# Transposes on TensorE whole or as pairs of 64-row blocks, and a new order of the operations

## The chip, the cores and the metric

The kernel runs on one core of one Trainium2 chip. The metric is the device time of one execution in microseconds; lower is better. The times of the kernel before are 197.99, 198.35 and 198.89 us, with a median of 198.35.

## The reference

Two stages follow each other. The first is a linear attention with a state of 40 x 40 for each of 4 batches and 8 heads over 768 steps; the second mixes tokens and channels of its output.

```python
for t in range(S):                                  # (B, H, S, D) = (4, 8, 768, 40)
    y[:, :, t] = np.einsum('bhd,bhde->bhe', rt, state)
    Sa = np.einsum('bhde,bhe->bhd', state, at)
    state_decay = state * wt[:, :, None, :] - np.einsum('bhd,bhe->bhde', Sa, bt)
    state = state_decay + np.einsum('bhd,bhe->bhde', vt, kt)
x = y.transpose(0, 2, 1, 3).reshape(B, S, H * D)    # (4, 768, 320)
theta = x @ w_theta
zr, zi = x * np.cos(theta), x * np.sin(theta)
u = x + np.einsum('ts,bsd->btd', w_tok_r, zr) + np.einsum('ts,bsd->btd', w_tok_i, zi)
out = u + np.maximum(u @ w_ch, 0.0)
```

## The kernel before

The 768 steps of a batch are cut into 6 chunks of 128 tokens, 24 chunks in all, numbered through the batches. For each chunk the kernel loads w, k, b, a, v and r (160 KB each), takes the logarithm of w on ACT (`lw`, L445), sums it over the chunk with a triangular matmul, and scales k, b and a with the exponentials (`kb` and `ah`, mostly on POOL). The scaled tiles are transposed on PE against an identity (`tkb`, `ta`, `tv`, `tr`, `to`, `tb`, and later `nut`, `xt`, `ut`, `wt`): a transpose is a matmul whose output lies in PSUM, and ACT or DVE copies it out (`ekb`, `ea`, `ev` and so on).

From the transposed tiles PE makes four score tiles for each chunk (`spsi`, `sphi`, `slv`, `slu`, L569). A score matmul contracts over 64 rows only, so two heads stand side by side in the upper and lower 64 rows of PE's array, each with a PSUM bank of its own. DVE multiplies a score tile with a mask (L578), or ACT copies it and POOL masks it. The recurrence of a chunk is then two steps, x0 (L616) and nu (L629), with a copy `nx` between them, a new state `gt` (L652), its transpose `gd` and the chunk's output y (L800, L802). The second stage adds theta, its sine and cosine (on ACT), the products z, the token mixing (`row`, L881, six steps of two 320-column matmuls a chunk) and the channel mixing (L763, L773). The token weights come as 12 tiles `wrow` of 128 x 768, loaded by DMAs that POOL issues (L960).

Nothing in this order comes from the loops. Each operation is recorded by `plan.add` with its number, what it reads and writes, and, where another engine could do it, an alternative (`alts`). Three tables decide: `ORDER` is the order in which all 1602 operations are issued, and since each engine works through its own instructions in order, it is the order on each engine and on SP's queue of loads and stores; `PICK` lists the operations that take their alternative; `HOMES` gives each PSUM tile its bank. PSUM has 8 banks. Banks 0 to 3 form two doubles (`ps_d`) for score tiles, and banks 4 to 7 are singles (`ps_s`) for all else:

```python
doubles = [psum.tile([128, 2, 512], FP32, name=f"ps_d{i}") for i in range(DOUBLE // 2)]
singles = [psum.tile([128, 512], FP32, name=f"ps_s{i}") for i in range(BANKS - DOUBLE)]
```

A fourth table, `WARM`, puts matmuls on a constant tile (`busy`, L1019) ahead of a few early operations. All but 11 of the 134 recorded transposes go through PE; the 11 of `CROSSBAR` are done by DMA.

Of the kernel before, what the change touches and what calls it, by code (L numbers as in the profile page):

```python
# [26 lines left out]
    0, 7, 3, 6, 1, 2, 20, 8, 21, 23, 24, 4, 27, 9, 32, 30, 5, 22, 31, 33, 12, 25, 26, 34, 11,  # L27
    28, 10, 69, 35, 36, 29, 70, 37, 18, 47, 44, 40, 19, 48, 72, 45, 38, 41, 71, 49, 73, 39, 46,
    98, 119, 76, 99, 58, 14, 42, 100, 74, 57, 15, 13, 120, 122, 101, 50, 121, 79, 75, 51, 123,
    53, 106, 102, 107, 131, 108, 80, 52, 16, 77, 109, 132, 125, 78, 43, 103, 81, 17, 110, 134,  # L30
    126, 111, 133, 82, 56, 84, 137, 54, 104, 124, 138, 112, 129, 83, 85, 87, 130, 88, 127, 55,
    156, 86, 128, 59, 157, 89, 146, 184, 143, 90, 147, 105, 158, 61, 97, 60, 139, 187, 159,
    135, 62, 144, 148, 164, 96, 188, 160, 165, 191, 140, 93, 136, 145, 161, 166, 141, 91, 185,
    167, 213, 186, 92, 194, 214, 149, 189, 142, 162, 168, 150, 215, 163, 169, 190, 216, 195,
    152, 221, 170, 234, 151, 246, 192, 222, 235, 193, 237, 217, 95, 236, 202, 238, 218, 94,
    196, 203, 197, 63, 241, 155, 247, 171, 267, 248, 219, 239, 199, 198, 172, 220, 223, 205,
    249, 200, 240, 271, 64, 244, 272, 242, 299, 245, 201, 154, 273, 224, 243, 300, 173, 301,
    261, 206, 254, 274, 302, 225, 174, 262, 303, 279, 153, 175, 258, 306, 176, 255, 212, 259,
    263, 280, 250, 177, 204, 281, 256, 211, 275, 496, 282, 260, 320, 226, 251, 305, 257, 208,
    252, 276, 264, 283, 253, 317, 207, 227, 349, 327, 265, 277, 497, 328, 304, 309, 278, 329,  # L40
    498, 284, 266, 310, 270, 499, 330, 350, 285, 307, 351, 268, 318, 286, 354, 308, 269, 331,
    352, 500, 311, 361, 332, 319, 287, 314, 353, 312, 209, 336, 333, 539, 362, 210, 337, 289,
    356, 288, 315, 363, 313, 322, 290, 364, 338, 355, 291, 387, 325, 292, 339, 316, 365, 540,
    388, 359, 366, 389, 541, 357, 360, 340, 390, 341, 382, 358, 391, 321, 116, 503, 113, 501,
    542, 412, 373, 181, 342, 334, 376, 374, 502, 392, 367, 411, 326, 504, 377, 375, 506, 335,
    393, 368, 505, 323, 178, 369, 545, 524, 394, 378, 370, 507, 517, 525, 413, 508, 372, 526,
    384, 371, 509, 395, 416, 396, 527, 532, 417, 528, 397, 510, 511, 514, 529, 544, 117, 595,
    512, 572, 533, 415, 383, 530, 118, 398, 573, 515, 596, 513, 554, 385, 399, 534, 531, 574,
    418, 597, 401, 535, 400, 516, 575, 414, 402, 543, 379, 324, 404, 114, 567, 598, 536, 403,
    546, 548, 115, 380, 581, 642, 576, 582, 555, 601, 549, 577, 381, 583, 599, 66, 386, 550,  # L50
    584, 537, 557, 568, 600, 551, 182, 522, 558, 602, 183, 585, 586, 538, 619, 578, 561, 587,
    419, 179, 518, 559, 547, 604, 519, 556, 427, 180, 428, 421, 429, 605, 560, 420, 606, 520,
    423, 552, 607, 626, 553, 562, 434, 422, 627, 564, 435, 425, 436, 565, 563, 643, 628, 424,
    437, 644, 610, 566, 629, 426, 613, 645, 603, 588, 611, 630, 231, 523, 571, 521, 589, 438,
    430, 570, 698, 635, 631, 646, 612, 439, 431, 636, 632, 440, 608, 745, 432, 614, 699, 647,
    609, 746, 700, 675, 648, 747, 637, 433, 615, 676, 616, 701, 293, 569, 633, 677, 748, 634,
    651, 649, 638, 678, 590, 652, 684, 296, 579, 685, 679, 617, 639, 228, 620, 621, 580, 653,
    706, 657, 591, 654, 680, 592, 618, 686, 650, 593, 661, 703, 687, 594, 441, 622, 711, 702,
    640, 442, 681, 712, 662, 688, 655, 658, 705, 656, 689, 659, 641, 663, 660, 682, 704, 664,
    690, 749, 667, 683, 665, 691, 68, 709, 692, 707, 67, 710, 729, 668, 65, 670, 672, 666, 708,  # L60
    694, 693, 750, 624, 695, 730, 719, 713, 697, 751, 720, 731, 696, 232, 732, 294, 233, 297,
    714, 721, 295, 733, 738, 298, 229, 734, 739, 715, 716, 230, 740, 735, 717, 754, 450, 752,
    451, 778, 755, 718, 346, 625, 452, 779, 453, 741, 343, 623, 756, 881, 780, 454, 757, 408,
    882, 781, 742, 405, 673, 671, 764, 883, 767, 765, 669, 782, 884, 444, 722, 455, 783, 443,
    768, 456, 766, 445, 784, 446, 736, 457, 885, 785, 458, 760, 737, 743, 447, 459, 753, 448,
    786, 787, 887, 744, 761, 796, 788, 769, 758, 460, 759, 789, 763, 461, 888, 762, 790, 462,
    797, 912, 463, 792, 791, 913, 793, 723, 770, 795, 892, 771, 914, 794, 674, 893, 915, 886,
    772, 802, 890, 464, 891, 803, 773, 347, 465, 916, 348, 344, 799, 917, 905, 805, 409, 345,
# [133 lines left out]
def mm(n):  # L202
    return max(n / 2.4 + 2.5, 25.0)
# [853 lines left out]
```

## Time and profile before

| | |
|---|---|
| median of the runs | 198.35 us |
| profiled execution, first to last instruction | 197.8 us |
| PE busy | 187.6 us (95%), 3288 matmuls |
| DVE busy | 164.3 us (83%) |
| ACT busy | 151.7 us (77%) |
| POOL busy | 145.1 us (73%) |
| HBM read and written | 29.54 MB and 3.93 MB |

Busy times of PE count a matmul from its start to its modelled end, so matmuls overlap. In a row of the chain of waits stand the start, the length and what took the time; the chain runs back from the last instruction to what released each one. A row of groups gives the count, the busy time, the mean of one in ns, and the idle time before it with what ended it.

### The profile page before, as it was taken

What the parts mean: (1) busy time and instruction counts of PE and PEld (TensorE: products, weight loads), DVE (VectorE), ACT (ScalarE), POOL (GpSimd) and SP (SyncE); (2) the same over time, 40 slices, a digit from 0 to 9 for tenths busy, and PEclk for the clock granted to TensorE, in tenths of its full rate; (3) what the DMA queues carried; (4) which work ended last, traced back from release to release, by engine and by line L of the source; (5) the groups of instructions that cost most, each with busy time, mean ns of one, the idle gap of its engine ahead of it and who ended that gap; (6) DMA issues with size and microseconds to landing.
All of it is one profiled execution on the core that took longest, in us unless ns stands there. A gap on an engine that the chain in (4) does not pass through costs nothing.

```text
span 197.8 us, 8019 instructions
## 1 busy us (share of the span) xinstructions
PE 187.6 (95%) x3288; PEld 150.3 (76%) x3288; DVE 164.3 (83%) x261; ACT 151.7 (77%) x337; POOL 145.1 (73%) x210
## 2 busy tenths in 40 slices
PE   7888999999989999999999999999999999999992
PEld 6776787777768788878878888888887878767661
DVE  5269899999989999888887988999999988675453
ACT  3584979799889988979988598888998986575111
POOL 8267544679879999699799939769699697558100
PEclk9999999999999999999999999999999999999999
DMA  6999879989999999999998899988998274863055
GB/s 119 210 212 163 154 161 196 182 166 197 233 174 173 207 171 185 190 185 223 153 210 168 153 187 170 188 148 169 182 155 163 43 177 102 87 194 104 0 191 174
DMA packets 134644, 32.75 MB, mean 166 GB/s; under 512 B 124816, under 2 KB 134608, under 8 KB 134608
## 3 DMA queue, kind: packets, MB, share of 16 engines
q1 hardware_dynamic: 131680, 29.19, 75.1%
q0 software_dynamic: 2784, 2.97, 9.6%
q8 instruction: 25, 0.41, 0.9%
q10 hardware_dynamic: 144, 0.08, 0.1%
q14 instruction: 11, 0.09, 0.1%
HBM read 29.54 MB, written 3.93 MB: 169 GB/s over the span
## 4 chain that ended last, share of the span: by engine, by line
PE 68%; DMA 9%; ACT 8%; SPq 6%; DVE 3%; issue 3%; POOL 1%; ACTq 0%; DVEq 0%; POOLq 0%
PE ps_s L881 17%; PE ps_s L391 10%; PE ps_d L569 9%; PE ps_s L763 5%; SPq L409 4%; DMA raw_w<-in_w_dram 3%; DMA raw_kb<-in_k_dram 3%; PE ps_s L711 3%; PE ps_s L652 2%; PE ps_s L629 2%; SPq L421 2%; DMA raw_r<-in_r_dram 2%; PE ps_s L538 2%; PE ps_s L773 2%; ACT cs L850 2%
## 5 line engine op out<-in xcount | busy, mean ns | idle before, releaser
L429 POOL TENSOR_TENSOR kb<-raw_kb,ex 128x320 bf16<-128x320 f32 x46 | 36.8, 811 | 9.7 <-DMA raw_kb<-in_k_dram 3.3
L881 PE MATMUL ps_s<-zr,wtok_r 128*128 128x320 bf16 x132 | 37.6, 299 | 0.0
L881 PE MATMUL ps_s<-zi,wtok_i 128*128 128x320 bf16 x132 | 37.5, 299 | 0.0
L578 DVE TENSOR_TENSOR lamu<-ps_d,mask_p 128x1024 bf16<-128x1024 f32 x22 | 26.8, 1219 | 1.7 <-PE ps_d L569 1.6
L578 DVE TENSOR_TENSOR psi<-ps_d,mask_p 128x1024 bf16<-128x1024 f32 x22 | 26.8, 1218 | 1.6 <-PE ps_d L569 1.4
L578 DVE TENSOR_TENSOR lamv<-ps_d,mask_p 128x1024 bf16<-128x1024 f32 x17 | 20.7, 1218 | 2.6 <-PE ps_d L569 1.8
L429 POOL TENSOR_TENSOR ah<-raw_a,we 128x320 bf16<-128x320 f32 x22 | 19.0, 866 | 3.6 <-DMA raw_a<-in_a_dram 1.6
L578 DVE TENSOR_TENSOR phi<-ps_d,mask_n 128x1024 bf16<-128x1024 f32 x17 | 20.7, 1218 | 0.9 <-PE ps_d L569 0.8
L865 POOL TENSOR_TENSOR zi<-cs,xp 128x320 bf16<-128x320 f32 x21 | 16.9, 816 | 3.3 <-ACT cs L850 3.3
L881 PEld LDWEIGHTS <-wtok_r 128*128 128x128 bf16 x144 | 14.0, 97 | 4.5
L569 PE MATMUL ps_d<-aT,kbT 64*128 64x128 bf16 x384 | 17.1, 217 | 0.2
L881 PEld LDWEIGHTS <-wtok_i 128*128 128x128 bf16 x144 | 14.1, 98 | 3.5
L391 PE MATMUL ps_s<-wide,kb 128*128 128x128 bf16 x184 | 15.0, 223 | 1.0 <-POOL kb L429 0.7
L865 POOL TENSOR_TENSOR zr<-cs,xp 128x320 bf16<-128x320 f32 x19 | 15.3, 810 | 0.7 <-ACT cs L850 0.7
L667 POOL TENSOR_TENSOR gt<-sum,ex 128x320 bf16<-128x320 f32 x13 | 9.5, 733 | 8.0 <-DVE sum L663 4.8
L800 PE MATMUL ps_s<-kb,lamv 128*128 128x40 bf16 x192 | 15.0, 180 | 0.0
L802 PE MATMUL ps_s<-kb,lamu 128*128 128x40 bf16 x192 | 14.9, 179 | 0.0
L569 PEld LDWEIGHTS <-kbT 64*128 64x128 bf16 x384 | 11.8, 94 | 3.1 <-ACT kbT L394 1.0
L800 PEld LDWEIGHTS <-lamv 128*128 128x128 bf16 x192 | 13.2, 96 | 0.6
L887 DVE TENSOR_TENSOR up<-ps_s,xp 128x320 bf16<-128x320 f32 x22 | 10.7, 488 | 3.5 <-PE ps_s L881 3.1
L435 POOL CAST r<-raw_r 128x640 bf16<-128x640 f32 x12 | 8.6, 720 | 6.5 <-DMA raw_r<-in_r_dram 6.5
L445 ACT ACTIVATE lw<-raw_w 128x320 bf16<-128x320 f32 x24 | 11.4, 475 | 2.6 <-DMA raw_w<-in_w_dram 2.6
(176 smaller groups left out, 606.7 us busy)
## 6 DMA issues: line engine op xcount, KB each, us to landing
raw_w<-in_w_dram SPq DMA_DIRECT2D x24, 160.0 KB, 4.1
raw_v<-in_v_dram SPq DMA_DIRECT2D x24, 160.0 KB, 3.9
raw_a<-in_a_dram SPq DMA_DIRECT2D x24, 160.0 KB, 4.2
raw_kb<-in_k_dram SPq DMA_DIRECT2D x24, 160.0 KB, 3.7
raw_kb<-in_b_dram SPq DMA_DIRECT2D x24, 160.0 KB, 4.0
raw_r<-in_r_dram SPq DMA_DIRECT2D x24, 160.0 KB, 4.4
out_dram<-oo SPq DMA_DIRECT2D x9, 160.0 KB, 2.0
wrow_i<-in_moe_w_tok_i_dram POOLq DMA_DIRECT2D x6, 192.0 KB, 5.3
```

Source lines behind the costliest of these rows:

```text
L391: nc.tensor.transpose(out=dst[:, c:c + 128], in_=pair(src, g), identity=ident)
L429: pool = ("POOL", lambda: nc.gpsimd.tensor_tensor(out=dst, in0=in0, in1=in1, op=ALU.mult))
L445: add("ACT", "ln", i, lambda: nc.scalar.activation(out=paired(lw)[:, :, :, 0:D], in_=paired(raw_w[s4]), func=AF.Ln), 473, [("raw_w", s4)], ...
L569: nc.tensor.matmul(t[:, q, g, :], lhsT=lhs[g][rows(q)], rhs=rhs[g][rows(q)], start=True, stop=True)
L578: add("DVE", kindm, i, lambda: nc.vector.tensor_tensor(out=flat, in0=whole(), in1=mask.to_broadcast([128, 2 * G, 128]), op=ALU.mult), 1217 ...
L667: add("POOL", "wgt", i, lambda: nc.gpsimd.tensor_tensor(out=new_state, in0=sum_t, in1=wm.to_broadcast([128, 8, D]), op=ALU.mult), 830, [(" ...
L763: nc.tensor.matmul(ps(pk)[:, 0:DM], lhsT=lhs[:, 3 * c + kt, :], rhs=wt[:, 3 * c + kt, :], start=kt == 0, stop=kt == 2, skip_group_check=n ...
L800: nc.tensor.matmul(o, lhsT=lamv[:, p, g, :], rhs=kb[:, 0, h, 0:D], start=first, stop=False, skip_group_check=True)
L802: nc.tensor.matmul(o, lhsT=lamu[:, p, g, :], rhs=kb[:, 1, h, 0:D], start=False, stop=True, skip_group_check=True)
L865: pool = ("POOL", lambda: nc.gpsimd.tensor_tensor(out=dst, in0=in0, in1=in1, op=ALU.mult))
L881: nc.tensor.matmul(acc(), lhsT=wtok[nm][j][:, s], rhs=zs[c][:, s], start=n == 0 and c == 0, stop=n == NT - 1 and c == 1)
L887: add("DVE", "uadd", q, lambda: nc.vector.tensor_tensor(out=u, in0=acc(), in1=x, op=ALU.add), 488, [pk, x_key(q)], [u_key(q)], at="row")
```

## The change

Transposes on PE get a second form. The new function `turned` replaces five places that each wrote a loop of `nc.tensor.transpose`; a transpose of 8-token runs (`turn_runs`) gets the same second form in place. Where `PICK` takes the alternative, the operation gets two neighbouring banks instead of one, and each block of 128 x 128 is transposed as two pieces of 64 rows, one into each bank. The copy out then reads both banks (`evac`). PSUM becomes one tile of 8 banks, so that any bank may be a single and any two neighbours a double:

```diff
-    doubles = [psum.tile([128, 2, 512], FP32, name=f"ps_d{i}") for i in range(DOUBLE // 2)]
-    singles = [psum.tile([128, 512], FP32, name=f"ps_s{i}") for i in range(BANKS - DOUBLE)]
+    banks = psum.tile([128, BANKS, 512], FP32, name="banks")
...
     def ps(key):
         h = plan.home[key]
-        return doubles[h[0] // 2] if len(h) == 2 else singles[h[0] - DOUBLE]
+        return banks[:, h[0]:h[0] + 2] if len(h) == 2 else banks[:, h[0]]
+
+    def split(key):
+        return len(plan.home[key]) == 2
...
-        for n in PICK:
-            self.ops[n].eng, self.ops[n].fn = self.ops[n].alts[0]
+        for n, m in PICK.items():
+            o = self.ops[n]
+            o.eng, o.fn = o.alts[m - 1][:2]
+            if o.eng == "PE":
+                o.new = (o.new[0], 2)
...
+    def turned(kind, i, key, srcs, reads, cost, at="tile"):
+
+        def go():
+            if not split(key):
+                t = ps(key).bitcast(BF16)
+                for m, src in enumerate(srcs()):
+                    nc.tensor.transpose(out=t[:, m * 128:m * 128 + 128], in_=src, identity=ident)
+                return
+            for m, src in enumerate(srcs()):
+                for c in range(2):
+                    nc.tensor.transpose(out=ps(key)[:, c].bitcast(BF16)[:, m * 64:m * 64 + 64],
+                                        in_=src[rows(c)], identity=ident[rows(c), rows(c)])
+        add("PE", kind, i, go, cost, reads, [key], at=at, new=(key, 1), tail=tail(128),
+            alts=(("PE", go),))
...
+    def evac(eng, kind, i, psk, dst, n, writes=(), part=None):
+
+        def copy(op, out, dt, w):
+            one, src = n * w // 64, ps(psk) if w == 32 else ps(psk).bitcast(BF16)
+            if not split(psk):
+                at = (part or 0) * one
+                op(out=out, in_=src[:, at:at + one])
+            elif part is not None:
+                op(out=out, in_=src[:, part, 0:one])
+            else:
+                op(out=out.rearrange("p (n c w) -> p c n w", c=2, w=w),
+                   in_=src[:, :, 0:one // 2].rearrange("p c (n w) -> p c n w", w=w))
```

`ORDER`, `HOMES` and `PICK` are new tables; the 1602 operations are the same. The first 21 operations stand as before, all others in a new order. `PICK` goes from 94 to 142 numbers. Of the 123 transposes on PE 31 are split (158 blocks). Some ninety copies, casts, products and masks change between ACT, DVE and POOL. The line of `PICK`:

```diff
-PICK = [
-    25, 31, 37, 39, 40, 48, 49, 75, 80, 85, 86, 115, 118, 130, 172, 180, 193, 203, 204, 222,
...
+PICK = {
+    25: 1, 31: 1, 37: 1, 39: 1, 40: 1, 48: 1, 49: 1, 60: 1, 75: 1, 80: 1, 88: 1, 89: 1, 115: 1,
```

Three places show how instructions move. The names in them are tiles with their buffer numbers: `psi` and `nuT` are score and transposed tiles of a chunk, `raw_*` the landing buffers of the loads, `wide` holds the identity.

On PE, the transposes of r for chunks 6 and 7. Before, they follow chunk 6's x0 step (L616):

```order
L616 MATMUL ps_s1_253<-v_2_134,psi_0_198 128x40
L538 LDWEIGHTS r_1_137
L538 MATMUL ps_s0_252<-wide_88,r_1_137 128x32x2x2
L538 LDWEIGHTS r_1_137
L538 MATMUL ps_s0_252<-wide_88,r_1_137 128x32x2x2
```

Now they follow chunk 5's last score tile (L603) directly, in 64-row pieces:

```order
L603 LDWEIGHTS nuT_1_197
L603 MATMUL banks_250<-rT_2_192,nuT_1_197 128x128
L572 LDWEIGHTS r_1_137
L572 MATMUL banks_250<-wide_88,r_1_137 128x16x2x2
L572 LDWEIGHTS r_1_137
L572 MATMUL banks_250<-wide_88,r_1_137 128x16x2x2
L572 LDWEIGHTS r_1_137
L572 MATMUL banks_250<-wide_88,r_1_137 128x16x2x2
```

Eight matmuls of 128 columns (32 x 2 x 2 in the output) became sixteen of 64 behind other 64-row work, and the x0 step moved ahead of the scores.

On ACT, around the logarithm of chunk 9's w. Before:

```order
L633 ACTIVATE nu_0_140<-ps_s1_253 128x8x40
L1024 ACT_TABLE_LOAD
L445 ACTIVATE lw_1_85<-raw_w_1_65 128x8x40
L394 COPY nuT_0_196<-ps_s2_254 128x256
L975 COPY wtok_i_0_240<-ps_s1_253 128x384
L622 CAST nx_1_207<-ps_s3_255 128x320
L394 COPY xT_0_220<-ps_s2_254 128x320
```

Now:

```order
L667 ACTIVATE nu_0_140<-banks_250 128x8x40
L1043 ACT_TABLE_LOAD
L514 ACTIVATE we_0_178<-sx_0_182 128x320
L422 COPY xT_0_220<-banks_250 128x320
L472 ACTIVATE lw_1_85<-raw_w_1_65 128x8x40
L422 COPY nuT_0_196<-banks_250 128x256
L656 CAST nx_1_207<-banks_250 128x320
L422 COPY wtok_i_0_240<-banks_250 128x384
```

Two operations moved ahead of the logarithm, and chunk 7's nx moved ahead of a copy of token weights; nuT and nx still stand behind the logarithm.

On SP's queue, the loads around chunk 9's w (`raw_w_1_65`). Before, it stands right behind chunk 8's b (`raw_kb_0_73<-in_b_dram`) and half of chunk 8's r:

```order
L409 DMA raw_kb_0_73<-in_b_dram 128x8x40
L421 DMA raw_r_0_80<-in_r_dram 128x1x320
L409 DMA raw_w_1_65<-in_w_dram 128x8x40
L409 DMA raw_kb_0_73<-in_k_dram 128x8x40
L421 DMA raw_r_0_80<-in_r_dram 128x1x320
```

Now:

```order
L436 DMA raw_a_4_72<-in_a_dram 128x8x40
L436 DMA raw_v_1_78<-in_v_dram 128x8x40
L436 DMA raw_kb_0_73<-in_k_dram 128x8x40
L448 DMA raw_r_0_80<-in_r_dram 128x1x320
L436 DMA raw_w_1_65<-in_w_dram 128x8x40
L436 DMA raw_kb_0_73<-in_b_dram 128x8x40
L448 DMA raw_r_0_80<-in_r_dram 128x1x320
```

Chunk 9's w is the 55th input load instead of the 52nd, and chunk 8's b the 56th instead of the 50th; chunk 9's a and chunk 8's v moved ahead of both.

More of the change, by code (lines that the diff above doesn't have):

```diff
@@ L508, in tr @@
             n = 4 * len(srcs)
[L509 to L510 removed]
+            turned(kind, i, p, lambda: pairs_of(srcs), skeys, n * mm(128))
             evac(eng, kinde, i, p, dst, n * 128, writes=[dkey])
@@ L706, in feature_major @@
         n = len(blocks)
-        def go():
-            t = ps(p).bitcast(BF16)
-            for m, src in enumerate(blocks):
-                nc.tensor.transpose(out=t[:, m * 128:m * 128 + 128], in_=src, identity=ident)
-        add("PE", kind, q, go, n * mm(128), skeys, [p], at=at, new=(p, 1), tail=tail(128))
+        turned(kind, q, p, lambda: blocks, skeys, n * mm(128), at)
         evac("ACT", kinde, q, p, dst[:, 0:n, :].rearrange("p a b -> p (a b)"), n * 128,
@@ L1015 @@
         if o.idx in WARM:
-            t = ps(o.new[0])
-            t = t[:, 0] if len(t.shape) == 3 else t
-            for _ in range(WARM[o.idx]):
-                nc.tensor.matmul(t[:, 0:128], lhsT=busy[:, 0:128], rhs=busy[:, 0:128],
+            at, n = WARM[o.idx]
+            for _ in range(n):
+                nc.tensor.matmul(banks[:, at, 0:128], lhsT=busy[:, 0:128], rhs=busy[:, 0:128],
                                  start=True, stop=True, skip_group_check=True)
```

80 lines of the change are left out of this document (32 added, 48 removed), and 236 rows, old and new, of tables (HOMES, ORDER, PICK).

## The prediction

> **What bounds the kernel now.** I read the page first, then busy time by stretch, then the chain that ended last, then the timeline around the places where the chain changes hands. Stretches first: start and end, PE, weight loads, DVE, ACT, POOL (instructions in brackets), granted clock, DMA share, GB/s.
>
> ```profile
> span 197.8 us, 8019 instructions
> PE 187.6 (95%) x3288; PEld 150.3 (76%) x3288; DVE 164.3 (83%) x261; ACT 151.7 (77%) x337; POOL 145.1 (73%) x210
> GB/s 119 210 212 163 154 161 196 182 166 197 233 174 173 207 171 185 190 185 223 153 210 168 153 187 170 188 148 169 182 155 163 43 177 102 87 194 104 0 191 174
> raw_w<-in_w_dram SPq DMA_DIRECT2D x24, 160.0 KB, 4.1
> wrow_i<-in_moe_w_tok_i_dram POOLq DMA_DIRECT2D x6, 192.0 KB, 5.3
> ```
> ```profile
> 0.00:57.00 57.00, 51.13 (x944) 41.72 (x945) 46.50 (x82) 43.29 (x104) 37.72 (x68) 1.00 0.94 181
> 57.00:180.00 123.00, 122.46 (x2238) 99.17 (x2234) 109.92 (x162) 105.11 (x227) 104.27 (x140) 1.00 0.89 164
> ```
>
> From 57 us on PE stands still for 0.5 us in 123; before that for 5.9 us in 57. The chain (start, us, what) says why:
>
> ```profile
> 13.29 5.87 DMA raw_kb<-in_k_dram
> ...
> 30.21 4.23 DMA raw_r<-in_r_dram
> ...
> 48.11 6.82 DMA raw_w<-in_w_dram
> ...
> 54.95 0.03 ACT lw L445
> ...
> 55.33 0.36 ACT nuT L394
> ...
> 55.73 0.44 PE ps_s L711 x5
> 56.17 0.24 PE ps_s L461
> 56.42 0.08 PE ps_s L464 x4
> 56.49 0.34 PE ps_d L569 x8
> 56.83 0.30 PE ps_s L629 x8
> ```
>
> Up to 55 us the input stream is the bound: three loads stand on the chain, the last is there at 54.93 (48.11 + 6.82), and PE follows it through ACT. From 55.7 on the chain is nearly PE alone. What ACT does there:
>
> ```profile
> 54.95 0.47 ACT L445 ACTIVATE lw<-raw_w 128x320 bf16<-128x320 f32 x1 [1.01 <-DMA raw_w<-in_w_dram]
> 55.33 0.35 ACT L394 COPY nuT<-ps_s 128x256 f32<-128x256 f32 x1
> 55.58 0.48 ACT L975 COPY wtok_i<-ps_s 128x384 f32<-128x384 f32 x1
> 55.95 0.44 ACT L622 CAST nx<-ps_s 128x320 bf16<-128x320 f32 x1
> ```
>
> ACT is in order: the logarithm of chunk 9 (L445) waits for its load, and chunk 7's nx behind it, so chunk 7's second step (L629) cannot start before that load. That is my pivot: 56.83 us. Behind it 141.0 us of span are left.
>
> How PE spends them:
>
> ```profile
> 103.68 0.30 PE L881 MATMUL ps_s<-zr,wtok_r 128*128 128x320 bf16 x1
> 103.81 0.30 PE L881 MATMUL ps_s<-zi,wtok_i 128*128 128x320 bf16 x1
> 103.95 0.39 PE L391 MATMUL ps_s<-wide,v 128*128 128x128 bf16 x4
> 104.17 0.20 PE L652 MATMUL ps_s<-v,kb 128*128 128x80 bf16 x1
> ...
> 104.38 0.20 PE L652 MATMUL ps_s<-v,kb 128*128 128x80 bf16 x1
> 104.42 0.20 PE L652 MATMUL ps_s<-nu,kb 128*128 128x80 bf16 x1
> 104.55 0.40 PE L569 MATMUL ps_d<-rT,vT 64*128 64x128 bf16 x8
> 104.80 0.39 PE L569 MATMUL ps_d<-rT,nuT 64*128 64x128 bf16 x8
> 105.12 0.19 PE L800 MATMUL ps_s<-kb,lamv 128*128 128x40 bf16 x1
> 105.16 0.18 PE L802 MATMUL ps_s<-kb,lamu 128*128 128x40 bf16 x1
> 105.18 0.18 PE L800 MATMUL ps_s<-kb,lamv 128*128 128x40 bf16 x1
> ```
>
> Ends are modelled, so I go by starts. A 320-column matmul takes 0.135 us, four 128-column transposes (L391) 0.22, so 0.055 each; an 80-column one 0.035, a 40-column one 0.025. Eight 64-row score matmuls (L569) take 0.25 us, 0.06 a pair: two of 128 columns run side by side in about the time of one. From the last L652 to the first L569 there are 0.13 us where 0.035 are needed: a change between 128- and 64-row matmuls costs 0.09. By these prices the matmuls that the order before has behind the pivot come to 133.1 us, changes included, against 141.0 in the span: 7.9 us are waits and the tail after the last matmuls.
>
> **The change part by part.** *Split transposes.* By the order, 31 of 123 PE transposes are split, 158 blocks, of which 133 stand behind the pivot. A split block is two 64-row matmuls of 64 columns in place of one of 128. No row has this shape. Upper bound: a pair costs as much as now, 0.06 (score pairs), +0.005 a block, 0.8 us in all. Lower bound: 64/128 of the whole block's 0.055, about 0.029, a gain of 0.026. I take 0.029, since the score pairs show that the partner is nearly free: 158 x 0.026 = 4.1 us on PE, 3.5 of it behind the pivot.
>
> The Trainium skill, TensorEngine Tiling (Array Packing), section Performance Considerations, speaks against this: it gives every matmul an overhead of some 60 cycles and advises not to tile a dimension that is already small. By that, a 64-column matmul stands near its floor and a pair would cost two floors. The row on the score pairs disagrees for 128 columns, where two share the time of one; for 64 columns no row decides.
>
> *Mode changes.* Runs of 64-row work go from 67 to 65, so 134 changes become 130: 4 x 0.09 = 0.4 us less. One split (chunk 4's kbT) even stands between 128-row neighbours.
>
> *Order behind the pivot.* The same prices on the new order give 129.8 us behind chunk 7's L629 step, against 133.1: 3.3 us less. (Over the whole order 4.5 less; the rest is work that would only wait for loads.)
>
> *Input stream ahead of the pivot.* The load of chunk 9's w goes from the 52nd input load to the 55th, chunk 8's b from 50th to 56th; in return one of the four wrow tiles that were issued between 45 and 50 us moves behind it:
>
> ```profile
> 45.01 0.60 POOL L960 DMA_DIRECT2D wrow_i<-in_moe_w_tok_i_dram  x1
> ...
> 49.18 0.59 POOL L960 DMA_DIRECT2D wrow_r<-in_moe_w_tok_r_dram  x1
> ```
>
> Three loads of 160 KB less one tile of 192, plus a 40 KB weight piece that now goes out first, are 328 KB, at 174 to 233 GB/s 1.4 to 1.9 us. The first two wrow tiles now stand behind chunk 5's ah product in POOL's order instead of chunk 6's products, so they go out among earlier loads that products wait for. Bounds: 0, if the stream has that much room at a share of 0.94, to the whole 5 us of R1 below. I take 1.4, by the rate of the slice in which the load landed.
>
> *Covers.* Where a copy stands between two PE steps, other matmuls have to fill the time.
>
> ```profile
> L394 ACT COPY kbT<-ps_s 128x512 f32<-128x512 f32 x15 | 8.9, 590 | 2.7 <-PE ps_s L391 2.3
> L394 ACT COPY aT<-ps_s 128x256 f32<-128x256 f32 x15 | 5.7, 381 | 0.4 <-PE ps_s L391 0.4
> L578 DVE TENSOR_TENSOR lamu<-ps_d,mask_p 128x1024 bf16<-128x1024 f32 x22 | 26.8, 1219 | 1.7 <-PE ps_d L569 1.6
> ```
>
> Chunk 21's kbT transposes now have only chunk 22's split ta and one score tile behind them, 0.12 + 0.22 us, before the scores that need the copy: 0.22 us of matmul end, 0.59 of copy and some 0.1 of signals leave about 0.5 us uncovered. Chunk 10's aT (copy 0.38) leaves 0.45, chunk 17's nuT 0.25, and chunk 8's scores take a bank whose lamu mask (1.22) is not done, 0.5. Together 1.7. Places of that kind in the old order (chunks 9 and 10) that now have more cover come to 0.9. I take +0.8; bounds 0 and 1.7.
>
> The Trainium skill, TensorEngine Tiling (Array Packing), section Restrictions and Gotchas, says that row tiling raises the pressure on PSUM, since row tiles need banks of their own. The order agrees: scores, splits and single tiles now share all 8 banks; its price in us is shown by no row.
>
> *Copies and engines.* A split block is copied out of two banks. The nearest rows, copies from two stretches of one bank and from one stretch,
>
> ```profile
> L546 ACT COPY rT<-ps_s 128x256 f32<-128x256 f32 x24 | 8.2, 378 | 1.6 <-DVE sx L482 0.8 <-PE ps_s L538 0.7
> L394 ACT COPY vT<-ps_s 128x256 f32<-128x256 f32 x21 | 7.6, 371 | 2.3 <-PE ps_s L391 1.2 <-PE ps_s L538 0.8
> ```
>
> differ by 7 ns, and 33 copies of that kind are 0.2 us on engines that have room. ACT goes from 327 to 321 operations, DVE from 236 to 244, POOL stays at 185: with 13 us idle on DVE between 57 and 180 I put this at nothing; were that cover gone, eight operations of 0.45 would cost 3.6.
>
> *Kept.* The first 21 operations and the warm-up matmuls stay: nothing.
>
> Sum: -3.3 + 1.4 + 0.8 = -1.1 us. The profiled execution took 197.8 us from first to last instruction, the runs' median is 198.35, 0.55 above it; I carry that along: 197.2 us.
>
> **The rivals.** *R1, slower: the stream.* If the two earlier wrow tiles (2 x 1.1 us at 174 GB/s) and all three loads (0.94 each) come in full ahead of chunk 9's w, the pivot moves by 5.0 and the time is 198.35 + 5.0 - 3.3 + 0.8 = 200.9. For it: the chain has three loads in 55 us. Against: a share of 0.94 leaves some room, and the tiles moved are the same bytes. It decides from 2.5 us on, so if that logarithm starts after 57.5 us.
>
> *R2, slower: a split pair costs two issues.* The 40-column rows start 0.025 apart; if 64 columns do the same beside each other, a pair costs 0.050, and 133 blocks lose 2.8 us of the gain: 200.0. Against: score pairs show no such spacing.
>
> *R3: the whole gain.* The stream holds the pivot where it was and the covers balance: -4.5 from PE, 193.9. For it: PE is busy 122.46 of 123. Against: in the first 57 us less PE work only waits longer.
>
> **How the numbers follow.** Forecast 0.48, R1 0.18, R2 0.10, R3 0.16, other mishaps or luck 0.08. The forecast's own range is 196.0 to 198.9 (stream 0.5 to 2.5, covers 0.4 to 1.4). Half a per cent, 1.0 us, is about what a measurement can tell. Half of the forecast lies below 197.4, most of the rest within; with R3 and half of the others that makes faster 0.44, same 0.25, slower 0.31. The range runs from R3 to R1: 193.9 to 200.9.
>
> **What would show it.** Right: transposes of 64 rows starting about 0.03 us a block; ACT's logarithm of chunk 9 one to two us later than 54.95; PE's stretch from chunk 7's second step to the end about 138.5 us (141.0 - 3.3 + 0.8). Wrong: that logarithm near 60 (R1), split blocks at 0.05 (R2), or waits of scores on copies and masks well above the 1.7 us counted here.

## The result and the profile after

The changed kernel took 201.13 us (median of 4 runs, 200.24 to 202.23), the kernel before 198.32 us (4 runs, 197.99 to 198.89). The ratio is 1.0137, with a 95% interval of 1.0093 to 1.018: slower by 2.8 us. The forecast was 197.2 us. Medians and ratios, here and below, leave out executions over 1.5% longer than the fastest of the same kernel; it matters most for the run e17, where 4 of 12 go and the median of all would be 200.42 us (1.0068 of before, all counted there too).

The profiled execution of the changed kernel took 201.11 us and spans 199.3 us. Its page, and three windows (stretch, length, busy us of each engine with the number of instructions, then TensorE's granted clock, DMA share and GB/s):

```profile
span 199.3 us, 8327 instructions
PE 183.4 (92%) x3446; PEld 146.7 (74%) x3446; DVE 163.4 (82%) x269; ACT 150.5 (76%) x331; POOL 145.4 (73%) x210
```
```profile
0.00:57.00 57.00, 48.27 (x931) 39.99 (x932) 44.08 (x82) 42.44 (x99) 37.16 (x67) 0.97 1.00 189
57.00:180.00 123.00, 120.80 (x2388) 97.42 (x2386) 109.84 (x168) 104.58 (x224) 104.34 (x138) 1.00 0.87 160
180.00:199.30 19.30, 14.35 (x133) 9.33 (x130) 9.51 (x21) 3.50 (x9) 3.85 (x6) 0.98 0.37 120
```

TensorE is busy 4.2 us less than before, as the splits were meant to make it, and the span is 1.5 us longer. Ahead of 57 us TensorE stands still for 8.7 us where it was 5.9; from 57 to 180 us for 2.2 where it was 0.5. So waits took more than the splits gave. They lie in three places.

**The first 36 us.** The second step of a chunk (L629 before, L663 after) closes the chain from one chunk to the next. Chunks 2 and 3 on TensorE, before:

```profile
26.11 0.36 PE L629 MATMUL ps_s<-nx,phi 128*128 128x40 bf16 x8
32.51 0.36 PE L629 MATMUL ps_s<-nx,phi 128*128 128x40 bf16 x8
```

and after:

```profile
28.45 0.36 PE L663 MATMUL banks<-nx,phi 128*128 128x40 bf16 x8
35.92 0.36 PE L663 MATMUL banks<-nx,phi 128*128 128x40 bf16 x8
```

The delay is 2.3 us at chunk 2 and 3.4 at chunk 3. At chunk 0 it was 0.1, so nearly all of the 2.3 arises around chunk 1's steps: its first step (L616 before, L650 after) starts at 20.59 us before and at 21.35 after, its second step at 21.95 and 23.95. The stretch in between, in the timeline before (start, us, engine, line, what):

```profile
20.75 0.58 ACT L394 COPY kbT<-ps_s 128x512 f32<-128x512 f32 x1 [0.23 <-PE ps_s L391]
21.39 0.62 PE L569 MATMUL ps_d<-aT,kbT 64*128 64x128 bf16 x16
21.93 1.23 DVE L578 TENSOR_TENSOR phi<-ps_d,mask_n 128x1024 bf16<-128x1024 f32 x1 [0.76 <-PE ps_d L569]
21.95 0.37 PE L629 MATMUL ps_s<-nx,phi 128*128 128x40 bf16 x8
```

and after:

```profile
22.64 0.69 DVE L422 COPY kbT<-banks 128x1024 bf16<-128x1024 bf16 x1 [0.66 <-PE banks L404]
23.39 0.62 PE L603 MATMUL banks<-aT,kbT 64*128 64x128 bf16 x16 [0.72 <-DVE kbT L422]
23.90 1.23 DVE L612 TENSOR_TENSOR phi<-banks,mask_n 128x1024 bf16<-128x1024 f32 x1 [0.57 <-PE banks L603]
23.95 0.37 PE L663 MATMUL banks<-nx,phi 128*128 128x40 bf16 x8
24.85 0.40 PE L404 MATMUL banks<-wide,nu 128*128 128x128 bf16 x4 [0.53 <-ACT nu L667]
```

Chunk 2's kb transposes stand later in TensorE's new order, their copy went from ScalarE to VectorE, and the scores that need it stand right behind. Chunk 1's second step is queued behind those scores. TensorE waits 0.72 us for the copy there, and every later step of the chain moves.

**The pivot.** The log of chunk 9's w (L472), chunk 7's nx behind it, and chunk 7's second step:

```profile
57.20 0.47 ACT L472 ACTIVATE lw<-raw_w 128x320 bf16<-128x320 f32 x1
57.57 0.36 ACT L422 COPY nuT<-banks 128x256 f32<-128x256 f32 x1
57.82 0.44 ACT L656 CAST nx<-banks 128x320 bf16<-128x320 f32 x1
58.32 0.37 PE L663 MATMUL banks<-nx,phi 128*128 128x40 bf16 x8
```

The pivot is 1.5 us late, but the log has no DMA behind its name: by the trace's record of that transfer, chunk 9's w had landed at 53.8 us, 3.4 us ahead of the log. ScalarE itself was late. What it did before, without a gap from 47.3 us on:

```profile
54.77 0.44 ACT L667 ACTIVATE nu<-banks 128x320 bf16<-128x320 f32 x1
55.22 1.28 ACT L1043 ACT_TABLE_LOAD   x1
56.52 0.47 ACT L514 ACTIVATE we<-sx 128x320 f32<-128x320 f32 x1
56.89 0.41 ACT L422 COPY xT<-banks 128x320 f32<-128x320 f32 x1
```

The first row reads chunk 6's second step, which starts 2.6 us later than before (54.36 against 51.80). The last two are the operations that moved ahead of the log; they take 0.68 us from 56.52 to its start.

**The end.** Waits of TensorE from 160 us on (waiting tile and line, releaser, us in total, times, longest), and the rows of two of them:

```profile
PE banks L603 <- DMA nuT<-nu: 1.0, 1, 1.0
PE banks L792 <- ACT uT L426: 1.0, 1, 1.0
PE banks L781 <- ACT uT L426: 0.4, 1, 0.4
```
```profile
168.77 1.23 SPq L731 DMA_TRANSPOSE nuT<-nu  x1
...
173.02 0.40 PE L603 MATMUL banks<-rT,nuT 64*128 64x128 bf16 x8 [1.04 <-DMA nuT<-nu]
```
```profile
194.03 0.56 DVE L934 SCALAR_TENSOR_TENSOR wrow_r<-banks,us 128x160 f32<-128x160 f32 x2
194.39 0.37 ACTq L938 DMA_DIRECT2D out_dram<-wrow_r  x1
194.62 0.33 SPq L938 DMA_DIRECT2D out_dram<-wrow_r  x1
194.80 0.32 ACT L426 COPY uT<-banks 128x192 f32<-128x192 f32 x1 [1.30 <-DVE wrow_r L934]
195.18 0.58 PE L792 MATMUL banks<-wch,uT 128*128 128x320 bf16 x3 [1.03 <-ACT uT L426]
```

A transpose by DMA, issued at 168.8, releases TensorE at 173.0. And ScalarE's queue holds the issue of a store (L938), which waits for VectorE's sum, ahead of the last copy of uT. Of the three waits only the one of 0.4 us was there before (0.3).

### The profile page after: what moved, and what is told of

It is laid out like the page before. It is cut to its first block, busy times and chain, and to the rows that moved or that the text cites. A ratio compares the mean times of both kernels' runs of the same rounds, so it can differ in the third digit from the quotient of the medians.

```text
span 199.3 us, 8327 instructions
## 1 busy us (share of the span) xinstructions
PE 183.4 (92%) x3446; PEld 146.7 (74%) x3446; DVE 163.4 (82%) x269; ACT 150.5 (76%) x331; POOL 145.4 (73%) x210
## 5 line engine op out<-in xcount | busy, mean ns | idle before, releaser
L910 PE MATMUL banks<-zr,wtok_r 128*128 128x320 bf16 x144 | 41.0, 300 | 0.0
L910 PE MATMUL banks<-zi,wtok_i 128*128 128x320 bf16 x144 | 40.9, 299 | 0.0
L612 DVE TENSOR_TENSOR lamu<-banks,mask_p 128x1024 bf16<-128x1024 f32 x23 | 28.1, 1221 | 4.6 <-PE banks L603 4.3
L612 DVE TENSOR_TENSOR psi<-banks,mask_p 128x1024 bf16<-128x1024 f32 x23 | 28.0, 1218 | 2.7 <-PE banks L603 2.6
L603 PE MATMUL banks<-aT,kbT 64*128 64x128 bf16 x384 | 18.2, 220 | 2.3 <-DVE kbT L422 0.7
L612 DVE TENSOR_TENSOR lamv<-banks,mask_p 128x1024 bf16<-128x1024 f32 x15 | 18.3, 1218 | 2.3 <-PE banks L603 1.4
L612 DVE TENSOR_TENSOR phi<-banks,mask_n 128x1024 bf16<-128x1024 f32 x15 | 18.3, 1219 | 2.1 <-PE banks L603 2.1
L603 PEld LDWEIGHTS <-kbT 64*128 64x128 bf16 x384 | 12.6, 96 | 5.3 <-issue 2.7
L829 PE MATMUL banks<-kb,lamv 128*128 128x40 bf16 x192 | 14.9, 180 | 0.0
L831 PE MATMUL banks<-kb,lamu 128*128 128x40 bf16 x192 | 14.8, 179 | 0.0
L472 ACT ACTIVATE lw<-raw_w 128x320 bf16<-128x320 f32 x24 | 11.4, 476 | 2.2 <-DMA raw_w<-in_w_dram 1.9
L831 PEld LDWEIGHTS <-lamu 128*128 128x128 bf16 x192 | 13.0, 96 | 0.0
```

Of the source, the lines that this page charges most:

```text
L472: add("ACT", "ln", i, lambda: nc.scalar.activation(out=paired(lw)[:, :, :, 0:D], in_=paired(raw_w[s4]), func=AF.Ln), 473, [("raw_w", s4)], ...
L603: nc.tensor.matmul(t[:, q, g, :], lhsT=lhs[g][rows(q)], rhs=rhs[g][rows(q)], start=True, stop=True)
L612: add("DVE", kindm, i, lambda: nc.vector.tensor_tensor(out=flat, in0=whole(), in1=mask.to_broadcast([128, 2 * G, 128]), op=ALU.mult), 1217 ...
L829: nc.tensor.matmul(o, lhsT=lamv[:, p, g, :], rhs=kb[:, 0, h, 0:D], start=first, stop=False, skip_group_check=True)
L831: nc.tensor.matmul(o, lhsT=lamu[:, p, g, :], rhs=kb[:, 1, h, 0:D], start=False, stop=True, skip_group_check=True)
L910: nc.tensor.matmul(acc(), lhsT=wtok[nm][j][:, s], rhs=zs[c][:, s], start=n == 0 and c == 0, stop=n == NT - 1 and c == 1)
```

## The experiments

Below, A is the ORDER of the changed kernel and B that of before; the diffs give the rule by which a table was made. Unless said otherwise an operation keeps the engine and the PSUM banks of the order it is taken from. Medians are in us; the ratio is to the kernel before on the same chip. The changed kernel itself has 1.0137.

| kernel | median | ratio, 95% interval |
|---|---|---|
| e11, the code alone | 198.59 | 0.9987, 0.9954 to 1.0020 |
| e3, no split | 204.40 | 1.0289, 1.0258 to 1.0319 |
| e8, loads as before | 204.20 | 1.0287, 1.0230 to 1.0345 |
| e5, first 440 as before | 201.20 | 1.0100, 1.0065 to 1.0136 |
| e6, first 440 changed | 204.71 | 1.0276, 1.0221 to 1.0332 |
| e7, first 260 as before | 202.50 | 1.0182, 1.0138 to 1.0227 |
| e9, e7 with changed loads | 201.98 | 1.0163, 1.0110 to 1.0216 |
| e10, e9 and the copy | 202.01 | 1.0153, 1.0093 to 1.0213 |
| e1, first 560 as before, banks given out anew | 215.89 | 1.0872, 1.0828 to 1.0916 |
| e2, the mirror of e1 | 215.48 | 1.0846, 1.0811 to 1.0881 |
| e4, the copy | 201.01 | 1.0120, 1.0083 to 1.0158 |
| e13, early moves | 201.38 | 1.0113, 1.0066 to 1.0160 |
| e14, e13 and the copy | 201.12 | 1.0099, 1.0060 to 1.0138 |
| e15, e14 and late moves | 200.54 | 1.0093, 1.0055 to 1.0130 |
| e17, e14 less one log | 199.47 | 1.0028, 0.9980 to 1.0076 |
| e12, B and eight splits | 201.28 | 1.0122, 1.0062 to 1.0182 |
| e16, e12, mixing later | 200.05 | 1.0053, 1.0018 to 1.0087 |
| e18, six splits | 199.62 | 1.0049, 1.0011 to 1.0087 |

### What the code and the splits cost

```diff
-ORDER, HOMES, PICK = those of the change
+ORDER, HOMES, PICK = those of before
```

> The changed code with the order, the engines and the banks of before in full, and no transpose split: what is left of the change is one PSUM tensor of eight banks in place of six tiles, and the generalised copies. If the code alone costs nothing: within 0.3 us of before, 198.3 to 199.0. Rival (one tensor adds waits that six tiles did not have): 1 us or more slower, 199.7 and up.

198.59 us, level with before. One PSUM tensor of eight banks and the more general copies cost nothing; what the change does to the time is order, banks, engines and splits.

```diff
-PICK = {n: 1 for all 142}
+PICK = {n: 1 for the 111 that are no transposes of TensorE}
```

> The changed kernel with all 31 split transposes whole again; order, engines and banks (the first of each pair) as changed. If a split block takes about 0.03 us where a whole one takes 0.055, and TensorE bounds everything behind chunk 7's second step: 2.5 to 4.1 us slower than the changed kernel, 203.6 to 205.2. Rival (a pair of 64-row blocks costs two issues, or its mode changes and two banks eat the gain): within 0.7 us of the changed kernel or faster, 200.0 to 201.8.

204.40 us, 3.3 above the changed kernel. The same six blocks of chunk 22 in e3 and, split, in the changed kernel:

```profile
196.02 0.51 PE L404 MATMUL banks<-wide,us 128*128 128x128 bf16 x6
```
```profile
192.84 0.35 PE L408 MATMUL banks<-wide,us 64*128 64x64 bf16 x12
```

The first is from e3, the second from the changed kernel. A single one lasts 0.22 and 0.19 us by their groups, so six blocks start over 0.29 us and twelve half blocks over 0.16: 0.058 a block whole, 0.029 split. Splits are worth what the first theory said, and in this order the time follows. (Some of it is not the blocks: by the records of both traces the changes between 128- and 64-row work go from 130 to 138, 0.7 us by the prediction's price.)

### The loads

```diff
-the first 74 input loads in A in the sequence of A
+the first 74 input loads in A in the sequence of B
```

> The changed kernel, in whose order only the first 74 input loads on the load queue stand in the sequence of before (chunk 9's w is the 52nd again, chunk 8's b the 50th). Theory A (engine covers, not the stream): within 0.7 us of the changed kernel. Rival R1 of the prediction (the moved loads make the log of chunk 9 late): 1 to 2.5 us faster, 198.6 to 200.2.

204.20 us: neither. Undoing the moved loads costs 3 us more. GpSimd waits for chunk 4's r at 32.6 us, and TensorE behind it:

```profile
32.58 0.72 POOL L462 CAST r<-raw_r 128x640 bf16<-128x640 f32 x1 [3.86 <-DMA raw_r<-in_r_dram]
...
34.02 0.87 PE L569 MATMUL banks<-wide,o 128*128 128x128 bf16 x8 [1.85 <-POOL o L462]
```

Chunk 9's w lands at 50.8 us in this trace and its log starts at 59.3, so that load alone decides nothing here. The moved loads as a whole are the sequence that this engine order asks for, not a loss of their own. Yet the stream is close behind. With the changed table of loads, chunk 9's w landed at 53.8 us in the changed kernel's trace, at 53.9 in e13's, 56.1 in e3's, 56.4 in e17's, 57.5 in e14's and 58.5 in e4's and e15's. In e4 the log waits for it, as it does in e15 and e17 (0.92 and 0.58 us):

```profile
58.52 0.47 ACT L472 ACTIVATE lw<-raw_w 128x320 bf16<-128x320 f32 x1 [1.53 <-DMA raw_w<-in_w_dram]
```

### The first part, spliced

```diff
-ORDER = A
+ORDER = B[:440] + [n for n in A if n not in B[:440]]
```

> The changed code with the first 440 of 1602 operations (up to about 59 us) exactly as before: their order, engines and PSUM banks, and no split among them; all others exactly as changed, with the changed banks. No operation has a new bank in this run. Theory A (the changed first part, up to chunk 7's second step, loses 2 us by covers and waits that the prediction put at nothing): TensorE's stalls in 20 to 40 us near 2.4 us, and 1.3 to 2.5 us below the changed kernel, 198.6 to 199.8. Theory B (the rest of the changed order is the loss): within 0.7 us of the changed kernel, 200.4 to 201.8.

201.20 us, the number of B, though the early part of the trace is as A has it. Chunk 3's second step is at 31.70 us (35.92 in the changed kernel) and chunk 7's at 56.10 (58.32). But the splice makes waits of its own at the seam, and later one for a transpose by DMA. TensorE's waits from 40 to 70 us, and from 160 us on:

```profile
PE banks L404 <- ACT nuT L422: 1.3, 1, 1.3
PE banks L404 <- POOL ah L456: 1.0, 1, 1.0
```
```profile
PE banks L792 <- DMA xT<-xp: 1.7, 1, 1.7
PE banks L792 <- ACT uT L426: 1.0, 1, 1.0
```

```diff
-ORDER = A
+ORDER = A[:440] + [n for n in B if n not in A[:440]]
```

> The mirror: the first 440 operations exactly as changed, with the five splits among them, all others exactly as before, banks included. Theory A: the delay of 1.3 to 2.5 us at chunk 7's second step stays to the end: 200.0 to 201.2. Theory B: 198.1 to 199.0, as before.

204.71 us: worse than either theory. The early delay stays in full (chunk 7's nx 2.2 us behind before, chunk 12's 3.4), the old order behind it gains nothing back, and 1.7 us of waiting for a uT transposed by DMA come on top.

```diff
-ORDER = A
+ORDER = B[:260] + [n for n in A if n not in B[:260]]
```

> As the first of this call, but only the first 260 operations (up to about 38 us) as before, banks included. If the uncovered scores, transposes and xT between 18 and 38 us are the delay (3.2 us more stall there): as low as with 440 operations, 198.6 to 199.8. If it is the stretch from 38 us to chunk 7's second step, its loads or its log: 200.4 or more.

202.50 us, the number of the second theory; but chunk 3's second step is at 32.76 us, and the loss comes from the seam at 38 us, with waits of 1.1 and 1.7 us that end at 40.98 and 47.60 us.

```diff
-the load queue as in e7
+the load queue as in A throughout
```

> The first 260 operations of TensorE, ScalarE, VectorE and GpSimd (up to about 38 us) as before, banks included; the load queue keeps the changed sequence, and all other operations are as changed. In the run with the first 260 of every queue as before the loads at the seam made three waits of 1.3 to 1.7 us between 41 and 50 us. Theory A (covers in 18 to 38 us lose the time): with the loads in their changed sequence these three waits are gone, chunk 6's second step is at 51 to 52.5 us instead of 54.3, and the time is 1 to 2.5 us below the changed kernel, 198.6 to 200.1. Rival (the changed rest needs the changed first part; a splice costs what it wins): 200.6 or more.

201.98 us. Chunk 2's second step is at 25.85 us, so engine order and banks alone remove its delay of 2.3 us, with the changed loads. At chunk 3 the loads do not fit the old engine order: TensorE waits 1.7 us for o, later 1.9 us for kb. The theory holds at chunk 2, but the time is the rival's: these two waits alone are more than was won.

```diff
-ORDER, HOMES = A, those of A
+ORDER = B[:560] + [n for n in A if n not in B[:560]]
+HOMES = for each tile, in order, banks whose last reader lies far back in the order, near those of A where that agrees
```

> The changed code with the first 560 of 1602 operations in the order of before (none of them split, with the engine choices of before) and all others in the changed order; banks of PSUM given out anew. Theory A (covers ahead of chunk 7's second step, which the prediction put at nothing, hold up TensorE in 20 to 57 us, and chunk 7's second step comes 2 us late): TensorE's stalls between 20 and 40 us fall back from 5.5 to about 2.4 us, the step starts near 57 us instead of 58.7, and the time is 1.3 to 2.2 us below the changed kernel, 198.9 to 199.8. Theory B (the late waits after 160 us, and whatever the rest of the new order costs, are the loss): within 0.5 us of the changed kernel, 200.6 to 201.6.

> The mirror of the run before it: the first 560 operations in the changed order with the changed splits and engines, all others in the order of before, unsplit. Theory A: the late step stays (start near 58.7 us), behind it the 141.0 us of before: 200.0 to 200.8. Theory B: the first part loses nothing, the waits after 160 us are gone: 198.0 to 198.8, as before.

215.89 and 215.48 us (e2 is the mirror, near the banks of B): neither theory holds. A place in the order says when a bank's reader is issued, not when it is done. In e1 one group of transposes stands behind a mask copy of 1.2 us in its bank:

```profile
84.33 1.21 DVE L612 TENSOR_TENSOR psi<-banks,mask_p 128x1024 bf16<-128x1024 f32 x1
...
85.59 0.35 PE L408 MATMUL banks<-wide,wrow_i 64*128 64x64 bf16 x12 [1.53 <-DVE psi L612]
```

All later splices (e5 to e9) kept every tile's bank.

### The first part, by eleven moves

```diff
 L612 TENSOR_TENSOR lamv_202<-banks,mask_p 128x1024
 L422 COPY aT_185<-banks 128x512
-L612 TENSOR_TENSOR lamu_204<-banks,mask_p 128x1024
 L705 TENSOR_TENSOR gt_142<-banks,ex_174 128x8x40
+L612 TENSOR_TENSOR lamu_204<-banks,mask_p 128x1024
...
-L718 CAST gd_209<-banks 128x320
 L656 CAST nx_206<-banks 128x320
+L718 CAST gd_209<-banks 128x320
```

The first five lines are on VectorE, the rest on ScalarE; the other nine are of this kind. One of them puts ScalarE's log of chunk 5's w five operations earlier.

> The changed kernel with eleven operations moved in its order, all before 45 us and none of them a load, a DMA or work of GpSimd: on TensorE slv of chunk 1 ahead of the scores of chunk 1's y, the kb transposes of chunk 2 ahead of the a transposes of chunk 2 and of three fillers, sphi of chunk 3 ahead of the y of chunk 3's neighbour; on VectorE the decay product of chunk 0 ahead of a mask copy; on ScalarE two copies nx ahead of an exp and of a gd copy, and four others by a place or some. Theory A (in the first 35 us the chain from one chunk's second step to the next bounds the kernel, and the changed engine order lengthens it): chunk 6's second step 1.5 to 2.5 us earlier than in the changed kernel, and the time 0.8 to 2.0 us lower, 199.1 to 200.3. Rival (loads bound that part anyway): within 0.5 us of the changed kernel.

201.38 us, no change that can be told: the rival's number. The second steps on TensorE, from each trace:

| chunk | before | code alone (e11) | changed | e13 | e17 |
|---|---|---|---|---|---|
| 2 | 26.11 | 26.42 | 28.45 | 27.55 | 27.39 |
| 3 | 32.51 | 32.61 | 35.92 | 35.70 | 34.47 |
| 6 | 51.80 | 51.10 | 54.36 | 54.09 | 52.87 |
| 7 | 56.76 | 56.00 | 58.32 | 58.06 | 57.51 |

e13 wins 0.9 us by chunk 2 and has 0.2 left at chunk 3. The moved log stops ScalarE for its load, so the rival's reason holds there, but only because this log was moved:

```profile
31.48 0.47 ACT L472 ACTIVATE lw<-raw_w 128x320 bf16<-128x320 f32 x1 [1.90 <-DMA raw_w<-in_w_dram]
```

```diff
-the last copy of uT behind the issue of the store (L938)
+the last copy of uT ahead of it
```

> The kernel before it with ScalarE's last copy of uT ahead of the last store but one of its queue. Theory A and C together: 0.8 to 1.5 us below the kernel before it, 198.0 to 199.2, level with the kernel before the change. Rival: within 0.4 us of the kernel before it.

201.12 us: within 0.4 us of e13, the rival's number.

```diff
-L472 ACTIVATE lw_85<-raw_w_65 128x8x40
 L496 ACTIVATE ex_174<-banks 128x328
...
 L718 CAST gd_208<-banks 128x320
+L472 ACTIVATE lw_85<-raw_w_65 128x8x40
```

Against e14, this log goes back to its place, and chunk 5's copy of r with it.

> As the run with the early moves and the copy, but ScalarE's log of chunk 5's w and the copy of chunk 5's r keep the places they have in the changed kernel (the log, moved ahead by five places, had waited 1.9 us there for its load). Theory A (engine order is the delay by 32 us, and the moved log had hidden the gain): chunk 3's second step ends 1 to 2 us earlier than with the moved log, and the time is 0.5 to 1.5 us below that run (201.3), 199.8 to 200.8. Rival (the loads bound chunks 3 to 7 in this order whatever the engines do before): within 0.4 us of it.

199.47 us, below the range of theory A; 1.0028 of before (0.9980 to 1.0076), so level with it. The interval lies clear below that of the changed kernel (1.0093 to 1.0180) and overlaps a little with e14's. Moves of nine operations in the first 45 us, and the copy at the end, take back most of the loss by this ratio, some half by the other one given for e17 (1.0068). At chunk 3 they take back 1.4 of the 3.4 us. In e17's trace the stream is what is late next: chunk 9's w lands at 56.4, and its log waits.

```profile
56.39 0.47 ACT L472 ACTIVATE lw<-raw_w 128x320 bf16<-128x320 f32 x1 [0.58 <-DMA raw_w<-in_w_dram]
```

### The end

```diff
+L426 COPY uT_223<-banks 128x2x3x32
 L938 DMA out_dram<-wrow_r_246 128x160
-L426 COPY uT_223<-banks 128x2x3x32
```

> The changed kernel with one operation moved: ScalarE's copy of the last uT ahead of the issue of the last store but one on the same engine, which waits 1.2 us for VectorE's sum. Theory C (in-order issue on ScalarE alone delays the last mixing step): TensorE's wait of 1.19 us ahead of the last mixing step falls to 0.1 to 0.3 us and the time falls by 0.6 to 1.2 us, 199.9 to 200.5. Rival (the copy is early but the last stores and their landing set the end): within 0.3 us of the changed kernel.

201.01 us: no difference that can be told. In the traces the wait of 1.03 us is gone, and from the start of VectorE's last sum u (L916) to the end of the span it is 5.8 us in e4, e14 and e17 against 7.0 in the changed kernel and e13. Two more pairs differ by this copy alone, e10 with e9 and e14 with e13:

> The kernel before it in this call, with ScalarE's last copy of uT ahead of the last store but one of its queue. Theory C (the tail loses 1.2 to 1.7 us to in-order issue on ScalarE): 0.9 to 1.7 us below the kernel before it. Rival: within 0.4 us of it.

202.01 against 201.98 (e9), and 201.12 against 201.38 (e14, e13). Three pairs give 0.1, 0.0 and 0.3 us where the traces of e4 and e14 show 1.2. In e10's trace this tail is 6.9 us against 7.0 in e9's: its last stores landed some 1 us later behind that sum than in e4's, so there nothing was won. In e4's trace chunk 9's w came 4.7 us later than in the changed kernel's; whether such things hide the gain in the other two pairs is open.

```diff
+L792 MATMUL banks<-wth,xT_220 128x320
 L910 MATMUL banks<-zr_231,wtok_r_237 128x320
...
-L792 MATMUL banks<-wth,xT_220 128x320
```

> The kernel before it with three more operations moved behind 170 us: TensorE's theta product of chunk 23 ahead of a row step, VectorE's sums of chunks 18 and 19 exchanged, one product of GpSimd later. If TensorE waits there for single results: 0.3 to 0.9 us lower than the kernel before it. Rival (the transposes by DMA that land near 173 us set that part): within 0.3 us of it.

200.54 us. The median is 0.6 below e14's, in the range of the first theory; the ratios, 1.0093 and 1.0099, say the rival. No effect can be told.

### Splits in the order of before

```diff
-PICK, HOMES = those of before
+PICK, HOMES = those of before, with kbT of chunk 12, uT of 0 and 6, xT of 8, aT of 8, 11 and 13, vT of 16 split
```

> As the run before it, with eight transposes behind chunk 7's second step split where the next bank is free anyway and no change of mode is added: 39 blocks, each 0.0266 us shorter, 1.04 us of TensorE work. If TensorE bounds that part and a split costs nothing beside: 0.7 to 1.1 us below the run before it, 197.5 to 198.1. Rival (the copies of two banks or the neighbours eat it): within 0.3 us of the run before it.

201.28 us: 2.7 above e11, where 1.0 below was expected. The 39 split blocks are 1.0 us less work for TensorE, and it waits more than that:

```profile
169.90 0.72 PE L792 MATMUL banks<-wch,uT 128*128 128x320 bf16 x4 [1.62 <-DMA uT<-up]
```

In e11's trace, the same order without the splits, no such wait stands there: there this transpose landed 2.6 us after its issue began, in e12 after 4.1. To see if the wait is the price:

```diff
-L792 MATMUL banks<-wch,uT_222 128x320
 L603 MATMUL banks<-rT_192,vT_194 128x128
...
 L910 MATMUL banks<-zi_232,wtok_i_244 128x320
+L792 MATMUL banks<-wch,uT_222 128x320
```

> Before's order with the eight splits, in which TensorE waited 1.6 us at 168 us for uT of chunks 12 and 13, transposed by DMA; here only the channel mixing of these two chunks (three TensorE steps and VectorE's two sums behind them) stands 2 us later in the order, behind chunk 23's first step and five row steps. Theory D (a transpose by DMA lands up to 4 us after its issue, and work that comes sooner waits for it: the splits' gain is handed to that queue): the wait falls below 0.3 us and the time by 1.0 to 1.8 us against the run with the eight splits alone (201.3), to 199.5 to 200.3 or less. Rival (the wait was one of that one execution): within 0.5 us of it.

200.05 us, 1.2 below e12; the wait is gone, though the transpose again took 4.1 us to land. Theory D holds for that part, with intervals of the two that overlap (from 1.0062 to 1.0087). What is left above e11 includes a split that waits for its second bank:

```profile
78.70 0.29 PE L408 MATMUL banks<-wide,ah 64*128 64x64 bf16 x8 [0.84 <-DVE phi L612]
```

```diff
-the transposes of a for chunks 8 and 11 split
+the same two whole
```

> The run with eight splits and the later channel mixing, without the two splits (transposes of a, chunks 8 and 11) ahead of which TensorE had waited 0.73 and 0.84 us, the second for the mask copy that still read the second bank: six splits are left, 0.83 us of TensorE work. Theory E (a split's price is its second bank, not its blocks): 0.5 to 1.3 us below the eight splits (200.2), 198.9 to 199.7 or less, and at best 0.5 us below before. Rival: within 0.4 us of the eight splits.

199.62 us. That is in the range of theory E, but the ratio is 1.0049 against 1.0053: the rival. The two waits are gone and others stand in their place, such as one for GpSimd's gated state:

```profile
148.17 0.20 PE L644 MATMUL banks<-gt,aT 128*128 128x80 bf16 x1 [0.41 <-POOL gt L701]
```

So with six splits, 0.83 us less of blocks, and the mixing moved, this kernel is 0.5% slower than before. No run has the moved mixing without splits, so what it costs by itself is open; by the records of the trace it adds two changes between 128- and 64-row work, 0.2 us. The traces suggest, and do not show, that in this order TensorE is not alone in setting the pace: a transpose by DMA, a bank and GpSimd each ended a wait where work had been saved. No kernel of this study is faster than before.

## Why the prediction was wrong

Point by point, against the profiled execution of before:

- *Split transposes, 0.029 us a block.* Right: 0.029. R2, a pair at two issues, falls by that row and by e3.
- *Order behind the pivot, 133.1 to 129.8.* Right. By the same prices the trace of after has 121.7 us of matmuls and 8.1 of mode changes behind the pivot, 129.8; the trace of before has 132.8. *Mode changes* alone went by nothing there, 88 to 90.
- *Input stream, +1.4.* The pivot did move by 1.5, for another reason, so that this term came out is luck. The log of chunk 9 started at 57.20, 2.25 behind before, just beyond the one to two us of the forecast and short of R1's 2.5, and its load had been there for 3.4 us. e8 shows that the moved loads as a whole were no loss. R1 did not hold in the profiled execution; in three others with the changed loads (e4, e15, e17) the load was last. How often it is in the changed kernel is open.
- *Ahead of the pivot, nothing.* This is the first step that failed. The sentence "in the first 57 us less PE work only waits longer" took that stretch as bound by loads alone, so covers were counted only behind the pivot. The chain from chunk to chunk bounds it too: 3.4 us late at chunk 3, 2.6 at chunk 6. There the kernel before waits for the load of chunk 9's w, which hides all but 1.5 of it in that execution. That it is the order of the engines is shown for chunk 2 (e9), and for 1.4 us at chunk 3 (e17); the rest there is open.
- *Covers, +0.8, bounds 0 to 1.7.* The second step that failed, and the largest in the sum. Waits and tail behind the pivot grew from 8.2 to 11.2 us, +3.0; TensorE's idle times there, as the traces have them, from 0.8 to 3.4. The four listed places (chunk 8's scores, aT of chunk 10, nuT of chunk 17, kbT of chunk 21) show 0.32, 0.23, 0.06 and 0.13, 0.7 where 1.7 was counted. What grew is a wait for a transpose by DMA (1.0, xT another 0.1) and the last copy of uT behind a store in ScalarE's queue (1.0). Neither was looked for: the prediction counted the copies' own durations and not what is queued ahead of them. The stretch from pivot to end is 141.0 us, not 138.5.
- *The level, 0.55 us.* The third. Every execution since has 1.65 to 2.0 us between its time and its span, most of them 1.7, so the execution of before with a span of 197.8 us would have taken some 199.5, not 198.35. Its pivot was late: e11, the same order, reaches it at 56.00. Against that the delay of the changed kernel is 2.3 us.

The sum with what was measured: pivot +1.5, work and modes -3.0, waits and tail +3.0, in all +1.5 for the two spans, and 1.1 for the level gives 2.6 of the 2.8 us. Of the 3.9 us between forecast and result the covers make 2.2, the level 1.1, the order 0.3 and the pivot 0.1. This account rests on one execution of each kernel: taking away the wait for the last copy (e4, e10, e14) gave 0 to 0.3 us of time and not 1.0, and no run takes back the whole loss for certain. So which steps failed is shown by the traces; how much of the median each is worth stays open in part. *R3*, the whole gain, needed that the covers balance; the +3.0 says that they do not, and e12 lost time by splits even in the old order.

## What to carry to other kernels

A stretch in which an engine mostly waits is not free: look for the chain that its waits belong to, and price a moved step there by what it delays, not by its work. In a tuned order other limits can lie close behind the first (here waits of 0.4 to 1.6 us for a DMA queue, GpSimd and a PSUM bank's last reader), so do not count a saving on the busiest engine in full before looking for the next one. Take the time of a profiled execution from the run it belongs to, and look for what stands ahead of a short copy in its own queue.

## What the runs showed of the hardware

- *Banks.* e1, a splice with the banks given out anew, took 215.89 us, e5, a shorter splice with every bank kept, 201.20. In e1's trace a bank is free when its reader's 1.2 us are over; that all of the 14 us comes from banks was not tested.
- *Transposes by DMA.* One takes the load queue 1.2 to 1.7 us to issue and landed 2.4 to 4.8 us after its issue began, in the same trace (e11: 160.46 to 162.88, 168.09 to 172.87).
- *The clock.* In e4 TensorE waited 1.79 us up to 59.30, and its granted clock (third number from the end) fell in the five us that follow:

```profile
55.00:60.00 5.00, 3.21 (x73) 2.62 (x70) 3.75 (x6) 3.42 (x7) 3.51 (x6) 0.97 1.04 212
60.00:65.00 5.00, 5.00 (x90) 3.92 (x86) 4.13 (x6) 3.54 (x10) 4.32 (x8) 0.69 1.08 198
```

 In e12 a wait of 1.62 us left it at 1.00:

```profile
170.00:175.00 5.00, 5.00 (x76) 3.57 (x77) 2.52 (x5) 3.12 (x5) 1.39 (x2) 1.00 0.74 210
```

 The Trainium skill, TensorE: Matmul & The Clock Gate, Part 1, gives an idle window of about 3.4 us after which the clock halves. In e4 the clock fell to 0.69 after about half of that, so the window is no safe margin here. Nor does the length of a single wait decide: in e9 the clock stayed at 1.00 from 30 to 40 us around a wait of 1.73 us that ended at 31.15, and was 0.75 from 45 to 50 us behind one of 1.92 us that ended at 43.61. In e8 it was 0.74 from 35 to 40 us behind the wait of 1.85 us. So part of what e8 and e9 lost is TensorE's time at the lower clock.
- *PSUM pressure.* The price that the prediction could not give for a second bank is a wait of 0.84 us in e16's trace, and without that split (e18) the time was no lower. The Trainium skill, TensorEngine Tiling (Array Packing), Restrictions and Gotchas, names the pressure; the trace agrees.
